# The 512-point transform as four products of 128 columns, with weight rows reordered at load and the instruction order from a table

## The chip, the cores and the metric

One core of one Trainium2 chip. TensorE (PE) multiplies matrices into PSUM, VectorE (DVE), ScalarE (ACT) and GpSimd (POOL) work on tiles, SyncE (SP) issues transfers; ACT and POOL issue some too. Every engine takes its own instructions in program order and waits on semaphores for the others. The metric is the device time of one execution in microseconds (us).

## The reference

A layer norm of x (2048 tokens, model dimension 512), and on it two branches whose sum is added to x: a filter in the frequency domain over both axes, and a gated feed-forward layer with 1792 hidden columns.

```python
def _A_ref(x, w_r, w_i):
    B, S, D = x.shape
    X = jnp.fft.rfft2(x.astype(jnp.float32), axes=(-2, -1))
    W = w_r + 1j * w_i
    X = X * W
    return jnp.fft.irfft2(X, s=(S, D), axes=(-2, -1)).astype(jnp.bfloat16)

def _B_ref(x, w_gate, w_up, w_down):
    g = jnp.einsum("bsd,df->bsf", x, w_gate)
    u = jnp.einsum("bsd,df->bsf", x, w_up)
    h = _gelu(g) * u
    return jnp.einsum("bsf,fd->bsd", h, w_down)

x = A_x
xn = _layernorm(x, axis=-1)
return x + _A_ref(xn, A_w_r, A_w_i) + _B_ref(xn, B_w_gate, B_w_up, B_w_down)
```

## The kernel before

**Order.** The kernel is written as some thousand tasks, each with an engine, a function that issues its instructions, what it reads and writes, an estimated length and a priority. `_Plan.schedule` goes through an assumed clock: whenever an engine is free it takes the ready task with the lowest priority number, gives PSUM banks to it, and so builds one list. `_Prog` turns the list into five queues with semaphore waits. Some tasks have a gate: they start only after a main product (gate/up or down) with at least that priority has started. The priorities come from the dictionary `K` and from the planned places of the main products (`gu_at`, `down_at`); `bonus` favours staying in the same TensorE mode (products on a half or a quarter of the array are modes of their own).

**Front.** Token tiles j = 0 to 15 are taken four at a time (block m). `ln_stat`, `ln_aggr` (L616 to L627) make mean and variance on VectorE and 1/std on POOL; for the first two tiles `ln_first` uses a square root on ScalarE. `ln_norm` (L641) scales a tile of 128 x 512 into `xn`, on VectorE or, for a few, ScalarE. `trans` (L649) transposes it on TensorE and copies it to `xnT[m]`, four quarters of the model dimension (dc) by 512 tokens.

**Transform along the model dimension.** `butter` (L679) folds the four quarters of `xnT[m]` on VectorE: sums and differences of the first and second half, of 1,024 elements each, then the sum and difference of the two quarters of the sums. `unit_D` (L688) multiplies, for each token tile, the folded quarters with constants `fd`: one product of 128 columns each for `f[0]` and `f[1]`, and two of 256 columns that accumulate for `f[2]` and `f[3]`. ScalarE evicts the bank to `xs`. `unit_A` (L707) does the first step along the tokens on half arrays; its results go through the DRAM scratch `scr1` to `tv`. Later `unit_B`, the multiplication with W, `unit_C`, a second scratch, `unit_E` and `unit_F` follow, and VectorE adds the result to `x_sb`.

**Feed-forward.** `gate_up` (L917) makes, for each group fc of 128 hidden columns, four products of 128 x 512 with `wg` and four with `wu`; one product per quarter dc. Blocks 0 and 1 do this directly; blocks 2 and 3 use `gate_up7` (seven products of half size per pair of groups), whose weight sums are made by `w_sums` and `w_sum4` on VectorE. The down products are `down` and `down_last`.

**Loads.** `load_w` (L570) loads a range of column groups of the gate or up weights, all four quarters, with one transfer: 128 partitions, four quarters, the columns. Ranges are 0 to 4, 4 to 8, 8 to 11 and 11 to 14, for gate and up: eight transfers, all on SP's queue (L586 to L607), among those of x, `ident`, `fd` (768 columns) and `am`. The first two tiles of x come half on SP's and half on ACT's queue.

Of the kernel before, what the change touches and what calls it, by code (L numbers as in the profile page):

```python
# [14 lines left out]
D = 512  # L15
# [14 lines left out]
def _constants():  # L30
# [9 lines left out]
    m64 = np.arange(64)[None, :]  # L40
    a0 = tp * (p + 0.5) * (4 * m64) / D
    a2 = tp * (p + 0.5) * (4 * m64 + 2) / D
    im0 = -np.sin(a0)
    im0[:, 0] = (-1.0) ** np.arange(P)
    fo = []
    for c in range(2):
        kodd = np.concatenate([4 * m64[0] + 1, 4 * m64[0] + 3])[None, :]
        a = tp * (p + P * c + 0.5) * kodd / D
        fo += [np.cos(a), -np.sin(a)]
    FD = np.concatenate([np.cos(a0), im0, np.cos(a2), -np.sin(a2)] + fo, 1)  # L50
# [70 lines left out]
    for i, (a, b) in enumerate(((c, s), (-s, c), (-c, -s))):  # L121
# [8 lines left out]
            f16(CM), f16(G.reshape(P, -1)), f16(NA))  # L130

# [83 lines left out]
class _Plan:  # L215
# [37 lines left out]
    def schedule(self):  # L253
# [26 lines left out]
        def refill():  # L280

            c = [i for i in range(8) if owner[i] is None and not isfull[i]]
            t = _Task()
            b = c[-1]
            t.i, t.eng, t.fn, t.r, t.w, t.over = len(T), "pe", (lambda e: self.fill(e, b)), (("wg", 0, 0), ("wg", 0, 1)), (("bank", b),), ()
# [136 lines left out]
def bass_parallel_sum__spectral_gfnet__glu_gated_geglu__prompt_kernel(  # L422
# [25 lines left out]
    with ExitStack() as es:  # L448
# [19 lines left out]
        tmp = area[:, 0:1024].rearrange("p (a c) -> p a c", a=2)  # L468
# [3 lines left out]
        AREA = [("tmp",)] + [("fold", i, k) for i in range(2) for k in range(3)] + [("xs", i) for i in range(4)]  # L472
# [79 lines left out]
        def act(fn, n, r, w, prio, over=(), **kw):  # L552
            return add("act", fn, r=r, w=w, over=over, occ=n / 1200 + 0.055, lat=n / 1200 + 0.24, prio=prio, **kw)
# [13 lines left out]
        def wkey(nm, fs, dcs=(0, 1)):  # L567
# [73 lines left out]
        def ln_norm(j, prio, eng="dve"):  # L641
            if eng == "act":
                act(lambda e: e.activation(xn[:, j % 4, :], x_sb[:, j, :], ACT.Identity, bias=nmr[:, j:j + 1], scale=rstd[:, j:j + 1]), 770,
                    [("x", j, 0), ("x", j, 1), ("nmr", j), ("rstd", j)], [("xn", j % 4)], prio)
                return
            add("dve", lambda e: e.tensor_scalar(xn[:, j % 4, :], x_sb[:, j, :], ag[:, j, 0:1], rstd[:, j:j + 1], ALU.subtract, ALU.mult),
                r=[("x", j, 0), ("x", j, 1), ("ag", j), ("rstd", j)], w=[("xn", j % 4)], occ=0.33, lat=0.47, prio=prio)

        def trans(m, dcs, jjs, prio, eng="dve"):  # L649
# [9 lines left out]
            pe(f, [P] * (len(dcs) * len(jjs)), [("ident",)] + [("xn", jj) for jj in jjs], [("ps", v), ("tr", m, dcs, jjs)], prio, alloc=(v, 1, False))  # L659
# [19 lines left out]
        def butter(m, prio):  # L679
            f = fold[m % 2]  # L680
            k = ("fold", m % 2)
            x = xnT[m]
            dve(lambda e: e.tensor_tensor(tmp, x[:, 0:2, :], x[:, 2:4, :], ALU.add), 1024, xk(m), [("tmp",)], prio, x=2)
            dve(lambda e: e.tensor_tensor(f[:, 2:4, :], x[:, 0:2, :], x[:, 2:4, :], ALU.subtract), 1024, xk(m), [k + (1,)], prio, x=2)
            dve(lambda e: e.tensor_tensor(f[:, 0, :], tmp[:, 0], tmp[:, 1], ALU.add), 512, [("tmp",)], [k + (0,)], prio, x=2)
            dve(lambda e: e.tensor_tensor(f[:, 1, :], tmp[:, 0], tmp[:, 1], ALU.subtract), 512, [("tmp",)], [k + (2,)], prio, x=2)

        def unit_D(j, prio):  # L688
            v = newbank()
            m = j // 4  # L690
            f = fold[m % 2]
            k = ("fold", m % 2)
            c = slice((j % 4) * P, (j % 4 + 1) * P)

            def fn(e):
                o = bank(v).rearrange("p (a r c) -> p a r c", a=2, r=4)
                e.matmul(o[:, :, 0, :], f[:, 0, c], fd[:, 0:128], start=True, stop=False, skip_group_check=True)
                e.matmul(o[:, :, 2, :], f[:, 1, c], fd[:, 128:256], start=False, stop=False, skip_group_check=True)
                e.matmul(o[:, :, 1::2, :], f[:, 2, c], fd[:, 256:512], start=False, stop=False, skip_group_check=True)  # L699
                return e.matmul(o[:, :, 1::2, :], f[:, 3, c], fd[:, 512:768], start=False, stop=True, skip_group_check=True)  # L700
            pe(fn, [P, P, 256, 256], [("fd",)] + [k + (i,) for i in range(3)], [("ps", v)], prio, alloc=(v, 1, False), full=True)
            x4 = xs[j % 4]
            act(lambda e: e.activation(x4.rearrange("p (a c r) -> p a c r", a=2, r=4),
                                       bank(v).rearrange("p (a r c) -> p a c r", a=2, r=4), ACT.Copy, scale=SC_D),
                512, [("ps", v)], [("xs", j % 4)], prio)
# [270 lines left out]
        def x_sums(m, prio):  # L976
# [4 lines left out]
            o = [("xn", i) for i in range(4)]  # L981
            dve(lambda e: e.tensor_tensor(T1, X[:, 0:2, hi], X[:, 0:2, lo], ALU.subtract), 512, xl + xh, [("xt", 0)], prio, x=2, over=o[:1])
            dve(lambda e: e.tensor_tensor(T3, X[:, 2:4, hi], X[:, 0:2, hi], ALU.subtract), 512, xh, [("xt", 2)], prio, x=2, over=o[2:3])
            dve(lambda e: e.tensor_tensor(T2, X[:, 2:4, hi], T1, ALU.subtract), 512, xh + [("xt", 0)], [("xt", 1)], prio, x=2, over=o[1:2])
            dve(lambda e: e.tensor_tensor(T4, X[:, 2:4, lo], T2, ALU.subtract), 512, xl + [("xt", 1)], [("xt", 3)], prio, x=2, over=o[3:])
# [339 lines left out]
        pr = _Prog(nc, es)  # L1325
        pl.emit(pr)
# [51 lines left out]
```

## Time and profile before

| | us |
|---|---|
| median of 3 runs | 178.47 (178.37 to 178.93) |
| the profiled execution | 177.96 |
| its span, first to last instruction | 175.8 |

| engine | busy us |
|---|---|
| PEld (weight loads, overlapping PE) | 124.0 |
| ACT | 115.9 |
| POOL | 60.1 |

The span is what the views of the trace divide; the 2.2 us between it and the execution lie around the instructions. Busy times are sums of records, and on PE and VectorE successive records overlap, so a record's length is longer than the distance to the next one. The granted TensorE clock was 0.999 of full speed. The transfer engines are sixteen; the share that a view gives is their mean. Up to about 22 us they move 270 to 320 GB/s (slices of 4.4 us) at a share near one.

### The profile page before, as it was taken

What the parts mean: (1) busy time and instruction counts of PE and PEld (TensorE: products, weight loads), DVE (VectorE), ACT (ScalarE), POOL (GpSimd) and SP (SyncE); (2) the same over time, 40 slices, a digit from 0 to 9 for tenths busy, and PEclk for the clock granted to TensorE, in tenths of its full rate; (3) what the DMA queues carried; (4) which work ended last, traced back from release to release, by engine and by line L of the source; (5) the groups of instructions that cost most, each with busy time, mean ns of one, the idle gap of its engine ahead of it and who ended that gap; (6) DMA issues with size and microseconds to landing.
All of it is one profiled execution on the core that took longest, in us unless ns stands there. A gap on an engine that the chain in (4) does not pass through costs nothing.

```text
span 175.8 us, 4162 instructions
## 1 busy us (share of the span) xinstructions
PE 169.7 (97%) x1580; PEld 124.0 (71%) x1580; DVE 151.5 (86%) x346; ACT 115.9 (66%) x193; POOL 60.1 (34%) x104
## 2 busy tenths in 40 slices
PE   7989999999999999999999999999999999999992
PEld 2557555557758854444787788887889998888881
DVE  2689799979798755699699899998999999999992
ACT  3625997779973223388853899889928699996200
POOL 2020205458816368888678100004145120000000
PEclk9999999999999999999999999999999999999999
DMA  3999996898867877575898942400022223100013
GB/s 77 308 319 309 267 266 182 242 296 223 192 134 111 165 202 194 146 228 151 205 258 234 237 124 60 123 0 0 6 60 56 69 60 84 39 0 4 0 30 90
DMA packets 20819, 25.26 MB, mean 144 GB/s; under 512 B 3232, under 2 KB 16928, under 8 KB 20544
## 3 DMA queue, kind: packets, MB, share of 16 engines
q1 hardware_dynamic: 17088, 17.21, 36.4%
q0 software_dynamic: 3120, 7.47, 18.2%
q10 hardware_dynamic: 592, 0.33, 0.7%
q8 instruction: 12, 0.20, 0.5%
q14 instruction: 7, 0.06, 0.1%
HBM read 18.70 MB, written 6.29 MB: 142 GB/s over the span
## 4 chain that ended last, share of the span: by engine, by line
PE 83%; DVE 9%; DMA 3%; SPq 2%; issue 1%; DVEq 0%
PE ps L930 25%; PE ps L1105 23%; PE ps L1011 20%; DMA x_sb<-in_A_x_dram 3%; PE ps L826 3%; PE ps L877 2%; PE ps L657 2%; PE ps L855 2%; SPq L560 2%; PE ps L805 1%; DVE hT L1038 1%; DVE hT L1042 1%; PE ps L699 1%; PE ps L700 1%; PE ps L717 1%
## 5 line engine op out<-in xcount | busy, mean ns | idle before, releaser
L930 PE MATMUL ps<-xw,wu 128*128 128x512 f16 (+1 forms) x128 | 29.3, 353 | 0.5 <-DMA wu<-in_B_w_up_dram 0.5
L930 PE MATMUL ps<-xw,wg 128*128 128x512 f16 (+1 forms) x128 | 29.0, 353 | 0.2 <-DVE xw L668 0.2
L934 ACT ACTIVATE gl<-ps 128x512 bf16<-128x512 f32 (+1 forms) x32 | 17.3, 546 | 17.7 <-PE ps L930 17.6
L862 POOL COPY bc<-tv 1x128 bf16<-1x128 bf16 x16 | 8.7, 558 | 39.6 <-ACT bc L861 39.6
L940 DVE TENSOR_TENSOR hT<-ps,gl 128x512 bf16<-128x512 f32 (+1 forms) x26 | 15.4, 602 | 6.5 <-PE ps L930 5.6
L930 PEld LDWEIGHTS ps<-xw,wu 128*128 128x128 bf16 x128 | 12.0, 98 | 11.3 <-DMA wu<-in_B_w_up_dram 0.7
L930 PEld LDWEIGHTS ps<-xw,wg 128*128 128x128 bf16 x128 | 11.9, 98 | 10.6 <-DMA wg<-in_B_w_gate_dram 0.6
L613 POOL DMA_DIRECT2D xw<-in_A_w_r_dram x28 | 16.2, 612 | 7.9 <-PE ps L930 5.0
L1024 ACT ACTIVATE gl<-ps 128x512 bf16<-128x512 f32 x28 | 17.1, 632 | 2.1 <-PE ps L1011 1.2
L613 POOL DMA_DIRECT2D xw<-in_A_w_i_dram x28 | 16.1, 601 | 3.7 <-PE ps L1105 2.5
L1011 PE MATMUL ps<-xn,ws 128*128 128x256 f16 x112 | 16.2, 273 | 0.0
L1011 PE MATMUL ps<-xn,wu 128*128 128x256 f16 x112 | 16.0, 273 | 0.0
L1011 PE MATMUL ps<-xw,wg 128*128 128x256 f16 x112 | 16.0, 273 | 0.0
L1105 PE MATMUL ps<-wd,hT 128*128 128x256 bf16 x112 | 13.6, 273 | 0.0
L617 DVE BATCH_NORM_STATS2 st<-x_sb 128x6 f32<-128x512 bf16 x16 | 10.5, 683 | 3.5 <-DMA x_sb<-in_A_x_dram 3.3
L1105 PE MATMUL ps<-wd,hs 128*128 128x256 f16 (+1 forms) x112 | 13.4, 273 | 0.0
L1105 PE MATMUL ps<-wdt,hs 128*128 128x256 f16 x112 | 13.1, 273 | 0.0
L626 POOL TENSOR_TENSOR rstd<-vpe,mhalf 128x4 f32<-128x4 f32 (+1 forms) x5 | 4.6, 923 | 23.0 <-DVE vpe L624 23.0
L1105 PEld LDWEIGHTS ps<-wd,hT 128*128 128x128 bf16 x112 | 10.6, 98 | 2.1 <-ACT bc L861 0.3
L1105 PEld LDWEIGHTS ps<-wdt,hs 128*128 128x128 f16 x112 | 10.8, 98 | 1.6 <-issue 0.2
L1105 PEld LDWEIGHTS ps<-wd,hs 128*128 128x128 f16 x112 | 10.8, 98 | 1.6 <-DVE mu L1140 0.2
L1011 PEld LDWEIGHTS ps<-xw,wg 128*128 128x128 bf16 x112 | 10.7, 98 | 1.6 <-issue 0.2
(132 smaller groups left out, 381.9 us busy)
## 6 DMA issues: line engine op xcount, KB each, us to landing
scr<-ta SPq DMA_DIRECT2D x32, 64.0 KB, 4.9
tv<-scr SPq DMA_DIRECT2D x8, 256.0 KB, 5.6
scr<-bc SPq DMA_DIRECT2D x16, 128.0 KB, 3.1
area<-scr SPq DMA_DIRECT2D x8, 256.0 KB, 4.2
xw<-in_A_w_r_dram POOLq DMA_DIRECT2D x28, 64.0 KB, 3.8
xw<-in_A_w_i_dram POOLq DMA_DIRECT2D x28, 64.0 KB, 3.6
x_sb<-in_A_x_dram SPq DMA_DIRECT2D x6, 256.0 KB, 10.4
out_dram<-x_sb SPq DMA_DIRECT2D x12, 128.0 KB, 2.3
```

What stands on the lines that cost most here:

```text
L560: return add(eng, lambda e: e.dma_start(dst, src), r=r, w=w, over=over, occ=occ, lat=kb / 1024 / rate, prio=prio, dma=True)
L613: add("pool", lambda e: e.dma_start(dst, src), r=r, w=w, over=over, occ=0.7, lat=kb / 1024 / 0.27, prio=prio, gate=prio, dma=True)
L617: add("dve", lambda e: e.bn_stats(st[:, j, :], x_sb[:, j, :]), r=[("x", j, 0), ("x", j, 1)] + behind, w=[("st", j)], occ=0.6, lat=0.75, pr ...
L626: add("pool", lambda e: e.tensor_tensor(rstd[:, sl], vpe[:, sl], mhalf[:, 0:n], ALU.pow), r=[("vpe", j) for j in js] + [("mhalf",)], w=[(" ...
L826: ins = e.matmul(bank(v, hh)[64 * kl:64 * kl + 64, 256 * z:256 * z + 256], cm[64 * hh:64 * hh + 64, 2 * H + z, kl, i, :], pp[i][64 * hh:64 ...
L862: add("pool", lambda e: e.tensor_copy(z[0:1, 1, :].rearrange("o (b q) -> o b q", b=2), z256[0:1, :].rearrange("o (b j q) -> o b j q", b=2, ...
L930: ins = e.matmul(bank(v)[:, 0:n], w_sb[nm][:, dc, fc * P:(fc + 1) * P], xnT[m][:, dc, c0:c0 + n], start=(dc == 0), stop=(dc == 3))
L934: act(lambda e: e.activation(gl[k][:, 0:n], bank(vs[0])[:, 0:n], ACT.Gelu_apprx_tanh), n, [("ps", v)], [("gl", k)], prio)
L940: dve(lambda e: e.tensor_tensor(o, bank(vs[1])[:, 0:n], gl[k][:, 0:n], ALU.mult), n, [("ps", vs[1]), ("gl", k)], ks, prio + K["dH"])
L1011: ins = e.matmul(bank(v)[:, 256 * q:256 * q + 256], W_, B0[:, dc, :], start=(first and q == 0 and dc == 0), stop=(dc == 1), skip_group_che ...
L1024: act(lambda e: e.activation(gl[k][:], bank(v), ACT.Gelu_apprx_tanh), 512, [("ps", v)], [("gl", k)], prio + K["aG"])
L1105: ins = e.matmul(bank(v)[:, 256 * t:256 * t + 256], A0[:, f, P * t:P * t + P], B0[:, f, :], start=(first and t == 0 and f == 0), stop=(f = ...
```

## The change

Four things change together.

1. The fold goes one step further. `butter` makes the differences' quarters too: it keeps the two half-size sums and differences in `tmp[0]` and `tmp[1]` and makes four results of 512 elements instead of two. `unit_D` is then four products of 128 columns, each with its own quarter of the bank and its own 128 columns of `fd`, which shrinks to 512 columns. The eviction reorders what it writes to `xs`.
2. For the fold to work, quarters 1 and 3 of the model dimension are held from the end, and all quarters with their halves of 64 so placed that rows match. `ln_norm` writes the even quarters with halves of 64 swapped and the odd quarters with each half backwards, in two instructions instead of one. The gate and up weights must have the same row order: `load_w` makes four transfers instead of one, two for the even quarters (64 partitions each, halves swapped) and two for the odd quarters (128 partitions, the source as two halves of 64 rows, each taken backwards). Ranges are now 0 to 4, 4 to 9 and 9 to 14, so 24 transfers instead of eight; the odd quarters of range 0 to 4 go on ACT's queue.
3. `x_sums`, the filling product and the lists of keys follow the new names.
4. After all tasks are made, their priorities and gates are replaced by a table, `ORDER` and `GATES`, in hundredths, and `bonus` becomes 1.0. The planner then builds the list from these.

```diff
-    a0 = tp * (p + 0.5) * (4 * m64) / D
-    a2 = tp * (p + 0.5) * (4 * m64 + 2) / D
...
+    r = np.arange(P)[:, None] ^ 64
+    ae, ao = tp * (r + 0.5) * 2 * m / D, tp * (r + 0.5) * (2 * m + 1) / D
+    im0 = -np.sin(ae)
     im0[:, 0] = (-1.0) ** np.arange(P)
...
+    FD = np.concatenate([np.cos(ae), im0, np.cos(ao), -np.sin(ao)], 1)
...
+ORDER = [
+    0, 30, 315, 100, 0, 0, 63, 0, 63, 189, 378, 315, 252, 189, 126, 252, 441, 504, 126, 465, 1134, 819, 567, 1386,
...
+]
+GATES = {274: 5622, 275: 5293, 276: 4319, 293: 2653, 294: 2740, 295: 2653, 296: 2999, 297: 3261, 298: 5207, 302: 4319, 484: 5871, 485: 7488, 486: 7488, 487:
...
-        def load_w(nm, lo, hi, eng, prio, dcs=(0, 1)):
+        def load_w(nm, lo, hi, eng, prio, odd=None):
-            src = (B_w_gate if nm == "g" else B_w_up).rearrange("(dc p) f -> p dc f", p=P)
+            src = (B_w_gate if nm == "g" else B_w_up).rearrange("(dc i p) f -> i p dc f", i=2, p=P)
             cs = slice(P * lo, P * hi)
-            ds = slice(2 * dcs[0], 2 * dcs[-1] + 2)
-            dma(eng, w_sb[nm][:, ds, cs], src[:, ds, cs], w=wkey(nm, range(lo, hi), dcs), prio=prio, kb=64 * len(dcs) * (hi - lo))
+            n = hi - lo
+            for a in range(2):
+                dma(eng, w_sb[nm][64 * a:64 * a + 64, ::2, cs], src[0][64 - 64 * a:128 - 64 * a, :, cs], w=[(k, f, a) for k, f, _ in wkey(nm, range(lo, hi), (0,))],
+                    prio=prio + 0.01 * a, kb=32 * n)
+            for i in range(2):
+                v = src[1][:, i, cs].rearrange("(a q) f -> a q f", a=2)[:, ::-1]
+                dma(odd or eng, w_sb[nm][:, 2 * i + 1, cs], v, w=[(k, f, 2 + i) for k, f, _ in wkey(nm, range(lo, hi), (0,))], prio=prio + 0.02 + 0.01 * i, kb=32 * n)
...
-        load_w("g", 0, 4, "sp", -99)
+        load_w("g", 0, 4, "sp", -99, "act")
...
-        load_w("u", 0, 4, "sp", -97)
-        load_w("g", 4, 8, "sp", -96)
-        load_w("u", 4, 8, "sp", -95)
+        load_w("u", 0, 4, "sp", -97, "act")
+        load_w("g", 4, 9, "sp", -96)
+        load_w("u", 4, 9, "sp", -95)
...
-        dma("sp", fd[:], c_fd.ap(), w=[("fd",)], prio=-93, kb=192)
+        dma("sp", fd[:, 0:512], c_fd.ap(), w=[("fd",)], prio=-93, kb=128)
...
-        load_w("g", 8, 11, "sp", -92)
-        load_w("u", 8, 11, "sp", -91)
+        load_w("g", 9, 14, "sp", -92)
+        load_w("u", 9, 14, "sp", -91)
...
-        load_w("g", 11, 14, "sp", -88)
-        load_w("u", 11, 14, "sp", -87)
...
+            xq = x_sb[:, j, :].rearrange("p (d i a c) -> p i d a c", i=2, a=2, c=64)
+            o = xn[:, j % 4, :].rearrange("p (d i a c) -> p i d a c", i=2, a=2, c=64)
+            for i, (xi, oi) in enumerate(((xq[:, 0], o[:, 0][:, :, ::-1]), (xq[:, 1], o[:, 1][:, :, :, ::-1]))):
...
-            dve(lambda e: e.tensor_tensor(tmp, x[:, 0:2, :], x[:, 2:4, :], ALU.add), 1024, xk(m), [("tmp",)], prio, x=2)
-            dve(lambda e: e.tensor_tensor(f[:, 2:4, :], x[:, 0:2, :], x[:, 2:4, :], ALU.subtract), 1024, xk(m), [k + (1,)], prio, x=2)
-            dve(lambda e: e.tensor_tensor(f[:, 0, :], tmp[:, 0], tmp[:, 1], ALU.add), 512, [("tmp",)], [k + (0,)], prio, x=2)
-            dve(lambda e: e.tensor_tensor(f[:, 1, :], tmp[:, 0], tmp[:, 1], ALU.subtract), 512, [("tmp",)], [k + (2,)], prio, x=2)
+            t, d = tmp[0], tmp[1]
+            dve(lambda e: e.tensor_tensor(t, x[:, 0:2, :], x[:, 2:4, :], ALU.add), 1024, xk(m), [("tmp", 0)], prio, x=2)
+            dve(lambda e: e.tensor_tensor(d, x[:, 0:2, :], x[:, 2:4, :], ALU.subtract), 1024, xk(m), [("tmp", 1)], prio, x=2)
+            for i, (s, op) in enumerate(((t, ALU.add), (t, ALU.subtract), (d, ALU.subtract), (d, ALU.add))):
+                dve(lambda e, i=i, s=s, op=op: e.tensor_tensor(f[:, i, :], s[:, 0], s[:, 1], op), 512, [("tmp", i // 2)], [k + (i,)], prio, x=2)
...
-                e.matmul(o[:, :, 0, :], f[:, 0, c], fd[:, 0:128], start=True, stop=False, skip_group_check=True)
-                e.matmul(o[:, :, 2, :], f[:, 1, c], fd[:, 128:256], start=False, stop=False, skip_group_check=True)
-                e.matmul(o[:, :, 1::2, :], f[:, 2, c], fd[:, 256:512], start=False, stop=False, skip_group_check=True)
-                return e.matmul(o[:, :, 1::2, :], f[:, 3, c], fd[:, 512:768], start=False, stop=True, skip_group_check=True)
+                for i in range(4):
+                    ins = e.matmul(bank(v)[:, P * i:P * i + P], f[:, i, c], fd[:, P * i:P * i + P], start=(i == 0), stop=(i == 3), skip_group_check=True)
...
+        for t, v in zip(pl.tasks, ORDER):
+            t.prio = v / 100
+            t.gate = GATES[t.i] / 100 if t.i in GATES else None
+        pl.bonus = 1.0
         pl.emit(pr)
```

In the table's order SyncE's first transfers are x tile 0 and tile 1 (first halves), x tiles 2 and 3 (first halves), `ident`, x tiles 2 and 3 (second halves), then the even quarters of wg and wu for groups 0 to 4; the odd quarters of later ranges stand between even ones, x, `fd` and `am`. The last odd load, the first odd quarter of wu for groups 9 to 14, follows x tiles 8 to 11. ACT's queue starts with its halves of x tiles 0 and 1, three odd loads, the first table load, the fourth odd load, and then the square root of tile 0.

More of the change, by code (lines that the diff above doesn't have):

```diff
@@ L467, in bass_parallel_sum__spectral_gfnet__glu_gated_geglu__prompt_kernel @@
         area = sb("area", [P, 8192], F16)
-        tmp = area[:, 0:1024].rearrange("p (a c) -> p a c", a=2)
+        tmp = [area[:, 1024 * i:1024 * i + 1024].rearrange("p (a c) -> p a c", a=2) for i in range(2)]
         fold = [area[:, 2048 + 2048 * i:4096 + 2048 * i].rearrange("p (a c) -> p a c", a=4) for i in range(2)]
@@ L471, in bass_parallel_sum__spectral_gfnet__glu_gated_geglu__prompt_kernel @@
         vv = area[:].bitcast(BF16).rearrange("p (l c) -> p l c", l=32)
[L472 removed]
+        AREA = [("tmp", 0), ("tmp", 1)] + [("fold", i, k) for i in range(2) for k in range(4)] + [("xs", i) for i in range(4)]
         ta = sb("ta", [P, 2048], F16)
@@ L658, in f @@
                 return ins
-            pe(f, [P] * (len(dcs) * len(jjs)), [("ident",)] + [("xn", jj) for jj in jjs], [("ps", v), ("tr", m, dcs, jjs)], prio, alloc=(v, 1, False))
+            pe(f, [P] * (len(dcs) * len(jjs)), [("ident",)] + [("xn", jj, i) for jj in jjs for i in range(2)], [("ps", v), ("tr", m, dcs, jjs)], prio, alloc=(v, 1, False))
             w = len(jjs) * P
@@ L980, in x_sums @@
             T1, T2, T3, T4 = xt
[L981 to L985, printed above, removed]
+            o = [[("xn", i, a) for a in range(2)] for i in range(4)]
+            dve(lambda e: e.tensor_tensor(T1, X[:, 0:2, hi], X[:, 0:2, lo], ALU.subtract), 512, xl + xh, [("xt", 0)], prio, x=2, over=o[0])
+            dve(lambda e: e.tensor_tensor(T3, X[:, 2:4, hi], X[:, 0:2, hi], ALU.subtract), 512, xh, [("xt", 2)], prio, x=2, over=o[2])
+            dve(lambda e: e.tensor_tensor(T2, X[:, 2:4, hi], T1, ALU.subtract), 512, xh + [("xt", 0)], [("xt", 1)], prio, x=2, over=o[1])
+            dve(lambda e: e.tensor_tensor(T4, X[:, 2:4, lo], T2, ALU.subtract), 512, xl + [("xt", 1)], [("xt", 3)], prio, x=2, over=o[3])
         un = [0]
```

34 lines of the change are left out of this document (14 added, 20 removed), and 51 rows, old and new, of tables (GATES, ORDER).

## The prediction

> **What bounds the kernel now.** I read the page's busy shares first, then the chain of work that ended last in order of time, then the stages (windows), and last the timeline and the transfers of the first 26 us.
>
> ```profile
> span 175.8 us, 4162 instructions
> ...
> PE 169.7 (97%) x1580; PEld 124.0 (71%) x1580; DVE 151.5 (86%) x346; ACT 115.9 (66%) x193; POOL 60.1 (34%) x104
> ...
> PE   7989999999999999999999999999999999999992
> ```
>
> ```profile
> 3.67 4.67 DMA x_sb<-in_A_x_dram
> 8.41 0.71 DVE st L617
> ...
> 12.84 4.53 PE ps L930 x36
> ...
> 17.48 0.11 PE ps L699
> 17.59 0.11 PE ps L700
> ...
> 24.96 0.89 PE ps L657 x16
> ...
> 172.46 0.42 DVE x_sb L1125
> ```
>
> The chain has start, times and length. To 12.84 us it runs through loads and the first layer norms; from 12.84 to 172.46 it is TensorE nearly without a hole (159.6 us), and then 3.3 us of last addition and store. So TensorE columns count one to one, everything else only where TensorE must wait for it. The profiled execution took 177.96 us, 2.2 us more than its span, and the median of the runs shown is 178.47, another 0.5 us up; I add 2.7 us to a span.
>
> **The transform (removed).** A unit of `unit_D` is two products of 128 columns and two of 256. The 256s take 0.11 each on the chain; sixteen transposes of 128 columns take 0.89 us, 0.056 each. Before: 2 x 0.056 + 2 x 0.11 = 0.33 us. After: 4 x 0.056 = 0.22 us. Over 16 units 1.76 us goes. A rule against it: the Trainium skill, TensorE: Matmul & The Clock Gate, section Back-to-back issue gap, gives 81 ns for sustained 128-column products with their weight loads. By that a unit would take 0.32 us and nothing would be gained; the 0.89 us for sixteen, each with its own weight load, speaks against it here, and I keep 0.056.
>
> **Vector work (added).** `butter` grows by two half-size operations per block, eight in all; the windows' columns are length, PE, PEld, DVE, ACT and POOL busy, clock, DMA share, GB/s:
>
> ```profile
> 14.44 0.41 DVE L685 TENSOR_TENSOR area<-area 128x512 f16<-128x512 f16 x1
> 14.77 0.42 DVE L686 TENSOR_TENSOR area<-area 128x512 f16<-128x512 f16 x1
> ```
>
> ```profile
> 12.80:26.00 13.20, 13.16 (x111) 8.66 (x111) 12.14 (x34) 10.42 (x21) 1.15 (x1) 1.00 1.07 279
> 26.00:40.00 14.00, 14.00 (x100) 7.54 (x99) 12.94 (x38) 10.58 (x17) 7.26 (x10) 1.00 0.85 244
> 40.00:53.00 13.00, 12.94 (x123) 8.89 (x122) 11.50 (x25) 11.82 (x20) 8.09 (x15) 1.00 0.77 178
> ```
>
> ```profile
> L668 DVE COPY xw<-ps 128x256 f16<-128x256 f16 x1 | 0.3, 293 | 0.0
> ```
>
> A record of 0.41 us is followed 0.33 us later by the next, so 0.08 us of each overlaps: 8 x 0.33 = 2.6 us. Twelve layer-norm scalings on VectorE become 24 of 256 elements; the nearest row (293 ns, so 0.21 us in a row) gives 2 x 0.21 - 0.33 = 0.09 each, 1.1 us. Four on ScalarE (815 ns, L643) become halves, some 0.2 us more each by its 384 ns rows of 256, 0.8 us. Writing backwards costs nothing: L887 does it in 414 ns, L886 without in 427. Cover: from 12.8 to 53 us VectorE is busy 36.6 of 40.2 us, but 97 records x 0.08 = 7.8 us of that is overlap, so 11.4 us are free, against 3.7 added. Cost zero; without the cover, 3.7 us. The eviction of `unit_D` now writes every second element; between nothing and a doubling of its 606 ns (16 x 0.6 = 9.7 us of ScalarE, which has 7.4 us idle in those windows). I take nothing: L887 shows no price for another stepped write.
>
> **Order (moved).** I read the table's numbers as the order on each engine. Passages through the half-array mode of `unit_A` become six instead of four; one costs about 0.1 us to enter and 0.1 to leave (in the timeline the last product of one starts at 47.23 and takes its 0.11, the next begins at 47.44). That is +0.4 us. At the front SyncE issues the transfers of x tiles 2 and 3 third and fifth instead of sixth and seventh, and ScalarE's queue gets three weight loads before its table load and one before its first square root:
>
> ```profile
> 2.09 1.28 ACT L579 ACT_TABLE_LOAD   x1 [2.09 <-issue]
> ...
> 4.36 0.29 ACT L632 ACTIVATE vpe<-ag,epst 128x1 f32<-128x1 f32 x1 [0.77 <-DVE ag L631]
> ...
> 7.46 1.91 PE L930 MATMUL ps<-xw,wg 128*128 128x256 f16 x16 [0.18 <-DVE xw L668]
> ```
>
> An issue on that queue takes 0.66 us (two in 1.32), so the square root slips to about 5.9 us, the first transposes by 1.2 us and the first gate product from 7.46 to about 8.5. Against that x tiles 2 and 3 come near 6.2 instead of 8.34, and TensorE need not wait until 12.84 to run closed. Net between -0.6 and +0.1 us; I take -0.3. SyncE's issues rise by 10 on net to the end of the loads, at 0.5 us each, behind a queue that waits for bandwidth anyway.
>
> **Weight loads (split): the term that decides.** Eight loads become 24: for each of six ranges two of even quarters (64 rows outermost) and two of odd quarters. An odd load's source is written as two halves, each of 64 rows taken backwards, so its description has an outermost count of **two**, against 128 at the destination.
>
> ```profile
> DMA packets 20819, 25.26 MB, mean 144 GB/s; under 512 B 3232, under 2 KB 16928, under 8 KB 20544
> ...
> tv<-scr SPq DMA_DIRECT2D x8, 256.0 KB, 5.6
> ...
> wg<-in_B_w_gate_dram SPq DMA_DIRECT2D x2, 512.0 KB, 5.4
> ```
>
> ```profile
> 4.40:8.80 4.40, 4.22 (x31) 2.40 (x30) 2.93 (x9) 2.68 (x6) 0.00 (x0) 1.00 1.00 309
> ```
>
> No transfer of before has fewer than 16 pieces outermost. The narrowest, `tv<-scr` and its sibling on `area` (16 transfers, 16 rows of 16 KB), account for 256 of the 275 packets of 8 KB or more: a transfer is cut at its rows and the rows are dealt out. How one is dealt whose two sides begin with 2 and 128 is not shown. The bounds: over all sixteen engines (the odd loads cost what the old ones did) or over two. I take two, because a common division of both sides at their outermost count has only two parts, and every full-rate row has a count that sixteen divides. The Trainium skill, DMA: Bandwidth & Descriptors, section Why a DMA increments its semaphore by 16 and not by 1, says the same: the number of engines is the largest up to 16 that divides the slowest dimension of both sides, and on these queues the lowest-numbered ones are used. No run here shows it yet.
>
> Price over two engines. Up to the last odd load of wu (the second quarter of groups 9 to 13), each of those two carries half of 1,792 KB of odd quarters, 896 KB, and a sixteenth of the rest (x 1,536, even quarters 1,792, am 256, fd 128, ident 32: 3,744 KB), 234 KB: 1,130 KB. An engine's pace: 309 GB/s at a share of 1.00 is 19.3 GB/s, 53 ns a KB; the highest slice of the first 26 us, 389 GB/s, is 24 GB/s, 42 ns:
>
> ```profile
> GB/s 0 0 0 147 197 138 61 296 389 323 173 304 377 373 372 358 353 369 233 233 231 234 309 357 335 325 347 286 204 238 220 271 329 339 359 356 207 251 176 211
> ```
>
> I take 47 ns, between them, as two engines have the memory to themselves: 53 us. Transfers start moving near 2.5 us; with 0.5 for the signal the last lands at 56. In the table's order TensorE may do ahead of it only 32 transposes (1.8), 17 products of 512 columns (0.86 each, 14.7), four units D (0.9) and two A (0.9): 18.3 us, of which before had done 4.4 at 12.84 (16 transposes, 32 half products). So after 56 us there remains 159.6 - 1.8 + 0.4 - (18.3 - 4.4) = 144.3 us. **Sum:** 56 + 144.3 + 3.3 = 203.6 us of span, + 2.7 = 206.3; I say **206**. By 42 ns it is 201, by 53 ns 213. Within that wait TensorE starves in steps: the first gate quarters late, then each range; the work between is short enough not to add up beyond the last one. Products after an idle start ran 0.43 us apart in the warm-up (2.06, 2.48, 2.91) instead of 0.22, so restarts may add 1 to 3 us: 216 at the top, 197 at the bottom if the waits of before (about 1 us) and some of the loads' tail go too.
>
> **Rivals.**
> *Faster: the odd loads are spread over sixteen.* Then loads are bandwidth bound as before (346 KB an engine by the same point, landing near 20 us, ahead of the product that needs it) and the rest counts: -1.8 + 0.4 - 0.3 = -1.7, **176.8 us**. For it: every load row of before runs at full rate. Against: none has such a shape.
> *No gain: as before that, but the front loses.* The square root's delay of 1.5 us reaches TensorE whole, because the x tiles meet ScalarE's new loads on the same engines: -1.8 + 0.4 + 1.5, **178.6 us**. Against: VectorE waits for x tiles 2 and 3 in before until 8.41, later than any of this.
> *Slower by little: only the first four odd loads matter.* If engines take up odd loads from several queues at once and the later ones stay ahead, TensorE starts after 4 x 64 KB on an engine, 12 us, plus as much of the other queue, near 26 us instead of 10: **193 us**.
>
> **Numbers.** Two engines: 0.82, with its own range 197 to 216. Only the front loads: 0.05. Spread, faster: 0.10. Spread, no gain: 0.03. The predicted time is the likeliest, 206; the range 192 to 216 leaves out the two spread cases and little more. 0.3% of 178.5 is 0.5 us, about what can be told from no change here: faster 0.10, same 0.03, slower 0.87.
>
> **What would show it.** Right: the odd wg and wu loads take 10 to 30 us to land, the DMA row falls from nines to a few tenths over the first 55 us with well under 150 GB/s, the PE row has holes there and the chain names DMA for wg and wu, while a unit D takes 0.22 us and the stage after 60 us looks like before. Wrong: DMA at nines to 20 us, TensorE closed from about 9 us, and a time near 177; then a count of two outermost does not confine a transfer.

## The result, and the profile after

The changed kernel takes **210.24 us** (median of 4 runs, 210.06 to 210.76) against 178.5 for the kernel before on the same chip: a ratio of 1.177, with a 95% interval of 1.173 to 1.182. The forecast was 206, with 192 to 216 as its range.

The page of the profiled execution after (210.16 us; 40 slices of 5.2 us):

```profile
span 208.2 us, 4199 instructions
...
PE 176.0 (85%) x1580; PEld 124.8 (60%) x1580; DVE 155.2 (75%) x366; ACT 118.6 (57%) x197; POOL 59.0 (28%) x104
...
PE   7350669507949999999999999999999999999993
...
PEclk9955559975999999999999999999999999999999
DMA  3434125255859978586756799754000055020013
```

The same last row of the kernel before (slices of 4.4 us):

```profile
DMA  3999996898867877575898942400022223100013
```

TensorE's row has holes over the first twelve slices, some 62 us, and none later. The granted clock is half in five of these slices, and the transfer engines, at nines up to 26 us in the kernel before, stand at one to five tenths over the first ten. The same stretch in the view of the transfers, first 70 us, 40 slices of 1.75 us:

```profile
DMA  0557517111581111169311141689238897428999
GB/s 0 153 141 212 146 46 204 47 49 49 142 205 52 49 49 52 35 157 214 84 49 55 45 119 57 194 211 251 68 107 241 181 329 222 123 65 315 344 314 239
```

Read the two rows together. Wherever the share is one tenth, the rate is 35 to 57 GB/s, most often 49. The highest slice of before, 389 GB/s over sixteen engines, is 24 a piece; 49 is twice that. So two engines work and fourteen stand idle. That was the forecast's deciding step, and the Trainium skill, DMA: Bandwidth & Descriptors, section Why a DMA increments its semaphore by 16 and not by 1, has the rule that these numbers agree with: the largest number of engines, up to sixteen, that divides the outermost count of both sides.

The trace also records each write to the semaphore that tells of a transfer's landing, though no view prints them. An even load has sixteen writes. Each of the twelve odd loads has three: one soon after its issue and two at the end (the last one, issued at 46.70, has them at 47.68, 59.27 and 59.70). And nearly every ordinary load has fourteen early writes and two late ones: for the x tiles issued at 46.05 fourteen by 50.40, the last two at 55.97 and 56.22. So it is one and the same pair of engines that all odd loads queue on, and every other transfer has two of its sixteen parts behind them.

TensorE's waits (total, times, longest), and its timeline at their ends (start, length, what; in brackets the idle time before and what ended it):

```profile
PE ps L991 <- DMA wg<-in_B_w_gate_dram: 16.5, 3, 9.0
PE ps L718 <- DVE rstd L690: 5.1, 1, 5.1
PE ps L991 <- DMA wu<-in_B_w_up_dram: 5.0, 2, 2.7
```

```profile
21.91 3.57 PE L991 MATMUL ps<-xw,wg 128*128 128x256 f16 x16 [7.25 <-DMA wg<-in_B_w_gate_dram]
...
48.17 1.86 PE L991 MATMUL ps<-xw,wg 128*128 128x512 f16 x4 [9.00 <-DMA wg<-in_B_w_gate_dram]
...
59.94 1.02 PE L991 MATMUL ps<-xw,wu 128*128 128x512 f16 x4 [2.68 <-DMA wu<-in_B_w_up_dram]
...
72.17 1.07 PE L718 MATMUL ps<-ident,xn 128*128 128x128 f16 x16 [0.33 <-DVE xn L707]
```

The first gate product starts at 21.91 instead of 7.46, and its sixteen records of 256 columns span 3.57 us where before they spanned 1.91: half the clock. The last odd load of wu lets TensorE go on at 59.94; from there to the end of the span are 148.3 us. Two instruction queues suffered too. SyncE's and ScalarE's own queues (an issue is mostly 0.6 us; the longest single one among the loads of the kernel before is 2.72):

```profile
11.44 6.14 SPq L613 DMA_DIRECT2D wg<-in_B_w_gate_dram  x1
...
20.14 9.55 SPq L613 DMA_DIRECT2D wg<-in_B_w_gate_dram  x2
...
35.67 7.21 SPq L613 DMA_DIRECT2D wu<-in_B_w_up_dram  x2
```

```profile
5.36 5.27 ACTq L613 DMA_DIRECT2D wu<-in_B_w_up_dram  x1
...
10.67 0.29 ACT L689 ACTIVATE vpe<-ag,epst 128x1 f32<-128x1 f32 x1 [3.89 <-issue]
```

Seven issues on SyncE's queue and one on ScalarE's are held for 3 to 6 us (the longest is the one at 11.44; the lines with x2 have two issues). They are not those of odd loads alone: the one at 11.44 is of an even load, and one below is of x tiles. Whatever follows in that queue waits too, whether or not it needs those weights: ScalarE's first square root (10.67 instead of 4.36) and, on SyncE, `fd`, `am` and the x tiles. The chain of waits that ended last runs through such a bystander:

```profile
47.28 3.81 SPq L613
...
51.13 10.52 DMA x_sb<-in_A_x_dram
...
62.28 0.68 DVE area L746
```

An x load is issued late and lands at 61.65, two of its parts behind the last odd load (fourteen of its semaphore writes come by 55.50, the last two at 60.76 and 61.65). VectorE has its statistics at the head of its queue until then, and the folds, layer norms and transposes of 72.17 stand behind it.

### The profile page after: what moved, and what is told of

The parts are those of the page before. It is cut to its first block, busy times and chain, and to the rows that moved or that the text cites. A ratio compares the mean times of both kernels' runs of the same rounds, so it can differ in the third digit from the quotient of the medians.

```text
span 208.2 us, 4199 instructions
## 1 busy us (share of the span) xinstructions
PE 176.0 (85%) x1580; PEld 124.8 (60%) x1580; DVE 155.2 (75%) x366; ACT 118.6 (57%) x197; POOL 59.0 (28%) x104
## 2 busy tenths in 40 slices
DMA packets 19883, 25.20 MB, mean 121 GB/s; under 512 B 3320, under 2 KB 15992, under 8 KB 19608
## 4 chain that ended last, share of the span: by engine, by line
PE 59%; SPq 24%; DVE 10%; DMA 5%; issue 2%
SPq L613 24%; PE ps L1072 20%; PE ps L1166 17%; PE ps L991 12%; DMA x_sb<-in_A_x_dram 5%; PE ps L887 2%; DVE hs L1155 2%; DVE st L674 1%; PE ps L916 1%; PE ps L938 1%; PE ps L866 1%; PE ps L718 1%; PE ps L760 1%; DVE xn L707 1%; PE ps L1181 1%
## 5 line engine op out<-in xcount | busy, mean ns | idle before, releaser
L991 PE MATMUL ps<-xw,wg 128*128 128x512 f16 (+1 forms) x128 | 29.9, 378 | 16.5 <-DMA wg<-in_B_w_gate_dram 16.5
L923 POOL COPY bc<-tv 1x128 bf16<-1x128 bf16 x16 | 7.9, 494 | 44.3 <-ACT bc L922 44.1
L1072 PE MATMUL ps<-xw,wg 128*128 128x256 f16 x112 | 16.5, 273 | 0.0
L1166 PE MATMUL ps<-wd,hT 128*128 128x256 bf16 x112 | 13.5, 273 | 0.0
L764 ACT ACTIVATE area<-ps 128x512 f16<-128x512 f32 x16 | 10.5, 749 | 2.4 <-PE ps L760 2.2
```

What stands on the lines that cost most here:

```text
L764: act(lambda e: e.activation(x4.rearrange("p (a c r) -> p r a c", a=2, r=2), bank(v).rearrange("p (r a c) -> p r a c", a=2, r=2), ACT.Copy ...
L923: add("pool", lambda e: e.tensor_copy(z[0:1, 1, :].rearrange("o (b q) -> o b q", b=2), z256[0:1, :].rearrange("o (b j q) -> o b j q", b=2, ...
L991: ins = e.matmul(bank(v)[:, 0:n], w_sb[nm][:, dc, fc * P:(fc + 1) * P], xnT[m][:, dc, c0:c0 + n], start=(dc == 0), stop=(dc == 3))
L1072: ins = e.matmul(bank(v)[:, 256 * q:256 * q + 256], W_, B0[:, dc, :], start=(first and q == 0 and dc == 0), stop=(dc == 1), skip_group_che ...
L1166: ins = e.matmul(bank(v)[:, 256 * t:256 * t + 256], A0[:, f, P * t:P * t + P], B0[:, f, :], start=(first and t == 0 and f == 0), stop=(f = ...
```

## The experiments

All are compared with runs of the kernel before on the same chip; a ratio is to these runs.

**Is it the shape of the loads? Sixteen parts, four parts.** One number in `load_w`:

```diff
-                v = src[1][:, i, cs].rearrange("(a q) f -> a q f", a=2)[:, ::-1]
+                v = src[1][:, i, cs].rearrange("(a q) f -> a q f", a=16)[:, ::-1]
```

> The changed kernel with the source of each odd load written as sixteen groups of 8 rows (each backwards) instead of two of 64; bytes, number of transfers, queues and table stay. The odd quarters' weight rows come in another order, so the feed-forward products are of other rows. Theory (a transfer is dealt over as many engines as divide the outermost counts of both sides): sixteen engines, the first 50 us run at 200 GB/s and more, the loads land by 22 us, 176 to 178 us. Rival (the reading backwards, or the number of 24 loads, is what is slow): 205 to 211 us as after.

Measured: **179.6 us** (178.71 to 181.18, 12 runs), ratio 1.005 (1.001 to 1.009). Its transfers in the first 60 us (slices of 1.5 us):

```profile
DMA  0389999999999999999999999995975888654467
GB/s 0 114 249 259 258 250 241 263 233 227 264 203 267 269 264 275 252 230 210 234 353 377 361 350 295 336 227 103 263 197 139 210 235 86 135 131 96 100 155 234
```

All sixteen engines, and 30.6 us gone, with the same bytes, the same number of transfers and the same table. In its trace every odd load has sixteen semaphore writes. Nothing else of the change can carry these 30.6 us. But the rest is not the gain that the rival promised (176.8) either; that is taken up below. With a=4:

> The same with four groups of 32 rows; again another row order in the odd quarters. Theory: four engines, plateaus near 4 x 24 = 97 GB/s where two gave 47 to 49; up to the last odd load each of the four carries 448 + 234 = 682 KB instead of 1,130, at the 24 GB/s seen 29 us, landing near 33 us, some 6 us after the table's order needs it: 181 to 188 us. Rival (backwards or number of loads): 205 to 211 us.

Measured: **194.76 us** (194.13 to 195.21), ratio 1.089 (1.083 to 1.095). The order of the three is right, the size is not. Its first 70 us:

```profile
DMA  0557892862594235899999863629799999859797
GB/s 0 152 139 180 216 209 85 231 145 94 158 229 130 99 108 145 237 203 208 207 193 233 216 160 123 180 85 313 252 302 302 187 169 203 268 159 269 145 96 166
```

The plateaus now lie at 85 to 108 GB/s and two to three tenths: four engines. Each odd load has one early semaphore write and four at its end. In its trace the last odd load of wu lets TensorE go at 44.52, and from there to the end of its span (192.8) are 148.3 us, to the tenth what the changed kernel has after 59.94. So the time follows the landing of that load one to one, and it was the landing that I set too early, in both. At the plateaus' pace (42 ns a KB) four engines with a quarter of 1,792 KB and the sixteenth of the rest, 682 KB, need 28.6 us and two with 1,130 KB need 47.5; with 3 us of start and signal that is 31.6 and 50.5. TensorE goes on 12.9 and 9.4 us later. The few engines did not stop in between: once the transfers have started no slice of either view falls under the digit of their share (one and two tenths), and the next odd load was always issued before the one ahead of it had landed (in the changed kernel the load that landed at 47.83 was issued at 31.58, and the next, which landed at 52.02, at 35.67). It is their pace that varied. An odd load of 160 KB is 80 KB for each of the two. One landed at 37.63, 3.18 us after the odd load issued just ahead of it (40 ns a KB, for the most part in slices of 49 and 55 GB/s). Another, at 47.83, needed 4.81 us (60 ns a KB), while other engines moved data too, 194 and 211 GB/s in all. From 3 us to the last landing (59.70, and 44.27 with a=4) it is 50.2 ns a KB for the pair with its 1,130 KB each and 60.5 for the four with their 682. So the few engines are slower when the others work as well; that they then share the memory is the likely reason, and no run shows it by itself.

**And the shape alone, in the kernel before?** `load_w` of the kernel before with three transfers a range, all on SyncE's queue: both even quarters as before, each odd quarter as two halves backwards (without the `rearrange` and the backward slice in the control).

```diff
-            dma(eng, w_sb[nm][:, ds, cs], src[:, ds, cs], w=wkey(nm, range(lo, hi), dcs), prio=prio, kb=64 * len(dcs) * (hi - lo))
+            dma(eng, w_sb[nm][:, ::2, cs], src[:, ::2, cs], w=[(k, f, 0) for k, f, _ in wkey(nm, range(lo, hi), (0,))], prio=prio, kb=64 * n)
+            for i in range(2):
+                v = src[:, 2 * i + 1, cs].rearrange("(a q) f -> a q f", a=2)[:, ::-1]
+                dma(eng, w_sb[nm][:, 2 * i + 1, cs], v, w=[(k, f, 1 + i) for k, f, _ in wkey(nm, range(lo, hi), (0,))], prio=prio + 0.02 + 0.01 * i, kb=32 * n)
```

> The kernel before with only the loads changed: even quarters in one transfer per range, odd quarters in one transfer each, with the source as two halves of 64 rows backwards, all on SyncE's queue; 24 transfers in before's own order. The odd quarters' rows are in another order than the reference has. Theory: two engines again, x tiles 12 to 15 and the last up weights come near 50 to 55 us, 195 to 206 us, without any of the transform's change or the table. Rival (the table's order or the transform brings the loss): 178 to 180 us.

> Control to the run before it: the same 24 transfers, in the same places, with the odd quarters' 128 rows in their plain order, outermost count 128. The computation is the reference's. Theory: within 1 us of before, 178 to 179.5 us, as issuing is hidden behind bandwidth. Rival (more transfers on the queue cost): 181 us or more.

Measured: **210.61 us** (210.36 to 210.69), ratio 1.178 (1.170 to 1.185), and for the control **179.66** (178.72 to 180.19, 10 runs), ratio 1.005 (1.002 to 1.008). The shape by itself makes the whole loss; that the time comes within 0.4 us of the changed kernel's is chance, since order and path differ. Both forecasts were somewhat low: what stands behind the odd loads in their queue was not in the first, and the control shows that 24 transfers in place of eight cost about 1.2 us by themselves. Where the time goes in b2 is in its TensorE timeline:

```profile
12.23 3.57 PE L933 MATMUL ps<-xw,wg 128*128 128x256 f16 x16 [5.08 <-DMA wg<-in_B_w_gate_dram]
...
34.79 0.29 PE L700 MATMUL ps<-fd,area 128*128 128x128 f16 x1 [6.47 <-DMA fd<-c_fd]
...
51.72 1.87 PE L933 MATMUL ps<-xw,wu 128*128 128x512 f16 x4 [4.96 <-DVE vpe L627]
```

The longest wait is for `fd`, a load of 128 full rows that has nothing wrong with it. It stood behind held issues in SyncE's queue (issued at 26.51, in the kernel before at 7.25), and then with two of its parts on the busy pair: fourteen had landed by 31.30, the last two came at 34.28 and 34.74.

**Is the confinement a property of the shape alone?** The changed kernel with the twelve odd loads issued by GpSimd:

```diff
-                dma(odd or eng, w_sb[nm][:, 2 * i + 1, cs], v, w=[(k, f, 2 + i) for k, f, _ in wkey(nm, range(lo, hi), (0,))], prio=prio + 0.02 + 0.01 * i, kb=32 * n)
+                dma("pool", w_sb[nm][:, 2 * i + 1, cs], v, w=[(k, f, 2 + i) for k, f, _ in wkey(nm, range(lo, hi), (0,))], prio=prio + 0.02 + 0.01 * i, kb=32 * n)
```

> The kernel after, with all twelve odd loads issued from GpSimd's queue instead of SyncE's and ScalarE's; shapes unchanged. Theory (the shape of a transfer, not the queue that issues it, sets how many engines carry it, and always the same two): within some 8 us of after, 202 to 214 us; SyncE's own loads may no longer be held up behind the odd ones, which can give back up to 8. Rival (the software queue deals a transfer out over its own choice of engines): 180 to 195 us.

Measured: **196.75 us** (195.45 to 197.41), ratio 1.099 (1.094 to 1.105): 13.5 us under the changed kernel, and outside what my theory allowed. Its page:

```profile
DMA  3899999986996957559478897460000334110013
GB/s 88 171 179 185 151 185 189 179 184 185 234 251 148 180 117 153 133 135 195 111 234 210 216 241 206 127 150 0 2 5 0 75 90 108 31 26 0 3 27 81
DMA packets 21587, 25.24 MB, mean 130 GB/s; under 512 B 6176, under 2 KB 17312, under 8 KB 21312
```

The engines are all busy from 5 us on, with the same two-part shape. So it falls that such loads always go to the same two engines; that holds on SyncE's and ScalarE's queues. The section of the Trainium skill named above has this too: on GpSimd's queue a transfer that is split k ways takes k neighbouring engines from a place that moves round from transfer to transfer. The mean share fits that; a single engine isn't shown. It is no cure, though. The engines are busy at 180 GB/s instead of 250 to 270, and packets under 512 bytes went from 3,320 to 6,176. Smaller packets at the same share are the likely reason for the 17 us that remain over a16; no run separates them from the late `ident` and first weights (TensorE waited 3.7 us for `ident` and 8.2 us for a load of wg here).

**Where did the transform's 1.7 us go?** With the loads out of the way the change should have won. First attempt: the changed kernel with one plain transfer a range, table kept for everything else; then with the removed columns put back, with the eviction written in a row, and without the table. In these and in the `transform` kernels below, it is the gate and up products whose weight rows then don't match the columns' order.

```diff
-            for a in range(2):
-                dma(eng, w_sb[nm][64 * a:64 * a + 64, ::2, cs], src[0][64 - 64 * a:128 - 64 * a, :, cs], w=[(k, f, a) for k, f, _ in wkey(nm, range(lo, hi), (0,))],
...
+            dma(eng, w_sb[nm][:, :, cs], src[:, :, cs], w=wkey(nm, range(lo, hi)), prio=prio, kb=32 * n)
```

> The kernel after, with every range of groups of wg and wu loaded by one transfer of 128 plain rows (6 transfers instead of 24, table kept for all the rest). The rows of the quarters then stand in another order than the transform's constants take. Theory (the four products of 128 do save 1.8 us, and sixteen-row loads gave it back through 18 more transfers at the front, as the control with plain rows lost 1.2 us): 176.5 to 177.8 us, first gate product before 8.2 us. Rival (the saving does not exist, or other parts of the change, the vector operations and the stretched eviction, eat it): 178.3 to 179.6 us even with few loads.

> The kernel of plain, with six products of 128 columns in unit_D instead of four (the last two done twice, so those outputs are doubled): the columns that the change removed are put back. Theory (columns count one to one on TensorE, 0.056 us a product): 16 x 2 x 0.056 = 1.8 us over plain. Rival one (the units stand where TensorE has slack): under 0.5 us over plain. Rival two (a product of 128 with its own weight load costs 81 ns, as the Trainium skill's TensorE: Matmul & The Clock Gate, section Back-to-back issue gap, has it): 2.6 us over plain.

> The kernel of plain, with the eviction of unit_D written in a row instead of to every second element (the columns of the transform then stand in another order). The eviction goes back from about 750 ns to about 610. Theory (ScalarE's 16 x 0.14 = 2.2 us hide behind TensorE except where one product waits for the area, 0.3 us in the trace): 0 to 0.5 us under plain. Rival (the longer eviction is what gives the saving back): 1 us or more under plain.

> The kernel of plain without the table: the order comes from the list scheduler's own due times, as in the kernel before. Theory (the table is worth nothing that stands out here): within 0.6 us of plain. Rival one (the table carries the gain): 1 us or more over plain. Rival two (the table is what gives the saving back: four loads on ScalarE's queue, six passages of the half-array mode): 1 us or more under plain.

Measured: 185.81 us (184.59 to 187.03), 188.01, 185.04 and 186.9, ratios 1.037 (1.032 to 1.043), 1.045, 1.033 and 1.042. The forecast for plain missed by 8 us and took the base away from the other three, whose differences to plain are +2.2, -0.8 and +1.1 us: the new base is 6 us slower than a16, with fewer transfers. VectorE's timeline of plain, and TensorE's:

```profile
18.23 0.69 DVE L672 BATCH_NORM_STATS2 st<-x_sb 128x6 f32<-128x512 bf16 x1 [5.45 <-DMA x_sb<-in_A_x_dram]
```

```profile
21.26 1.03 PE L989 MATMUL ps<-xw,wg 128*128 128x256 f16 x4 [4.69 <-ACT gl L993]
```

VectorE's queue had the statistics of x tile 4 at its head and stood 5.45 us until it landed; the products `hT` behind it free the banks that TensorE waited for. In plain this x tile was issued behind five of the six weight loads and landed at 18.2; in a16 the wait ahead of that block's first statistics is 1.00 us. The table alone is not the reason, since the hole is there without it too. The edit itself may be: it keeps `kb=32 * n`, from which the planner reckons how long a transfer takes, for transfers of four times that size, so its list counts on weights and x tiles that come too early. No run changes that number alone; the kernels below give it right (128 KB a group), and their longest hole is 1.78 us. The hole at this place is 4.7 us in plain, 6.6 in plain_six, 6.0 in plain_evict, and 5.8 in plain_no_table, so the differences between the four say nothing on columns, eviction or table: inconclusive.

Second attempt, a cleaner base: the kernel before, its loads and its scheduler, with the transform alone changed; with the columns put back; and with the statistics placed as in before.

```diff
-                for i in range(4):
+                for i in (0, 1, 2, 3, 2, 3):
```

```diff
-                ln_stat(4 * m + i, a + i)
+                ln_stat(4 * m + i, a + i, [("xn", 2, 1)] if m == 2 else [])
```

> The kernel before with the transform alone changed (four products of 128, the two more vector operations per block, the layer norms in halves, the eviction to every second element): loads, their order and the scheduler as before, no table. The rows of the quarters then stand in another order than the transform's constants take. Theory (1.76 us of columns go, and VectorE's and ScalarE's extra work stays hidden): 176.3 to 177.6 us, that is 1.2 to 2.2 us under the runs of before beside it. Rival (the extra work on VectorE and ScalarE, 3.7 and 3 us, comes through at TensorE's waits for evictions and layer norms): 178 us or more, no gain.

> The kernel of transform, with six products of 128 columns in unit_D instead of four (the last two done twice, so those outputs are doubled), in the same order. Theory (columns count one to one): 1.8 us over transform, about the time of before. Rival (the units stand where TensorE waits anyway): under 0.6 us over transform.

Measured: **179.89 us** (179.09 to 181.16), ratio 1.007 (1.002 to 1.011), and 181.07, ratio 1.012 (1.007 to 1.017). The transform alone is no gain; it is 0.3 to 2 us slower. The theory's own half holds on TensorE: in the trace of transform four units start at 18.09 and the next work at 18.99, 0.90 us, where before they take from 17.21 to 18.53, 1.32 us (the first two lines below are transform, the others before). That is 1.7 us over the kernel.

```profile
18.09 1.07 PE L754 MATMUL ps<-fd,area 128*128 128x128 f16 x16
18.99 1.03 PE L985 MATMUL ps<-xw,wu 128*128 128x512 f16 x4
```

```profile
17.21 0.22 PE L697 MATMUL ps<-fd,area 128*128 128x128 f16 x1
...
18.53 1.03 PE L930 MATMUL ps<-xw,wu 128*128 128x512 f16 x4
```

With two more products each, the time rose by 1.2 us, in the right direction, but the two intervals overlap. What eats the saving showed first as one hole, 1.78 us in front of the transposes at 30.65, behind a wait of VectorE for x tiles:

> The kernel of transform, with the statistics of x tiles 8 to 11 placed behind the first layer norms of tiles 4 to 7 on VectorE, as they stand in the kernel before. In the trace of transform VectorE waited 2.46 us at the head of its queue for those x tiles, the layer norms stood behind, and TensorE lost 1.78 us in front of the transposes at 30.65. Theory (the transform does save 1.7 us, and this wait gave it back): 177.2 to 178.3 us, 1.2 to 2.2 us under transform, and no hole over 0.6 us ahead of the second block's transposes. Rival (the longer vector work is the cause, and the wait only moves to another place): within 0.6 us of transform, with another hole of a microsecond or more.

Measured: **180.38 us** (179.61 to 181.51, 12 runs), ratio 1.009 (1.006 to 1.013), against 179.89 with the hole. The hole went down to 0.23 us and nothing was won in the median; the profile that showed the hole was the slowest of transform's six runs (181.16), and how long it is in the others isn't recorded. TensorE's waits in this kernel:

```profile
PE ps L712 <- DVE xn L701: 1.0, 3, 0.5
PE ps L754 <- DVE area L742: 0.6, 2, 0.4
PE ps L1160 <- DVE hT L995: 0.4, 1, 0.4
PE ps L910 <- DVE hT L1093: 0.4, 1, 0.4
PE ps L1160 <- DVE wdt L1129: 0.3, 1, 0.3
PE ps L985 <- DVE hT L995: 0.3, 1, 0.3
```

Six lines of waits for VectorE, 3.0 us, at layer norms, folds and evictions; with one lesser it is 3.2 us after the first instruction, against 1.0 us in the kernel before. That is 2.2 of the 3.6 us by which transform_stats misses the saving (1.9 over before instead of 1.7 under); for the rest these lines have no place. The rival holds in the main: the wait moves to other places, if not as one hole of a microsecond. The groups of the changed kernel show what grew, and the three lines of before under them what it replaced (count, busy us, mean ns):

```profile
L764 ACT ACTIVATE area<-ps 128x512 f16<-128x512 f32 x16 | 10.5, 749 | 2.4 <-PE ps L760 2.2
...
L707 DVE TENSOR_SCALAR xn<-x_sb,ag,rstd 128x256 f16<-128x256 bf16 x24 | 6.9, 339 | 0.7 <-POOL rstd L683 0.7
...
L704 ACT ACTIVATE xn<-x_sb,nmr,rstd 128x256 f16<-128x256 bf16 x8 | 4.3, 592 | 0.0
```

```profile
L703 ACT ACTIVATE area<-ps 128x512 f16<-128x512 f32 x16 | 8.4, 610 | 0.8 <-PE ps L700 0.8
...
L646 DVE TENSOR_SCALAR xn<-x_sb,ag,rstd 128x512 f16<-128x512 bf16 x12 | 4.7, 412 | 0.4 <-POOL rstd L626 0.3
...
L643 ACT ACTIVATE xn<-x_sb,nmr,rstd 128x512 f16<-128x512 bf16 x4 | 3.0, 815 | 0.0
```

Half a layer norm costs 82% of a whole one on VectorE and 73% on ScalarE. The eviction's growth is that of its write: in plain_evict, written in a row, it takes 600 ns, in plain 746.

## Why the prediction held, and where it was off

**The shape (two of sixteen): right, and shown.** Plateaus of 49 GB/s, two late semaphore writes of each odd load, the loss in b2, its disappearance in a16. The rival that spreads the loads has a16 as its case.

**The landing: right mechanism, size 4 us short.** I had 53 us of transfer and a landing at 56; TensorE went on at 59.94. The load itself landed at 59.70. The term that was mis-sized is the pace: 47 ns a KB, taken between the bounds of 42 and 53, was 50.2 in the mean, and 3.2 ns on 1,130 KB are 3.6 us. The pair did have the memory to itself on the plateaus, at 42, but not while the other fourteen engines moved their parts. For a4 I took the quick bound of 42 for the whole way, where 60.5 was measured; that made the forecast 7 us too low.

**What is left after it: right.** 144.3 + 3.3 = 147.6 us forecast, 148.3 found, in two kernels. The forecast's 2.7 us around the span were 2.0 to the median. 203.6 + 3.9 + 0.7 + 2.0 is the 210.2.

**Which wait ends last: only half seen.** I priced the queue's odd loads and took the others as mere bystanders ("behind a queue that waits for bandwidth anyway"). In the trace the last x tiles of the block land 1.7 us after the last odd load is in use, held in the queue and with two parts behind it on the pair, and the chain goes through them. Had the odd load come at 56 and these x tiles as they did, TensorE would have run dry before the transposes of 72.17. That is read from the trace, not tried.

**The front.** The square root was forecast at 5.9 and came at 10.67, as ScalarE's fourth odd load held its queue for 5.27 us, not 0.66. It hid behind the gate weights, which came only at 21.91. What the front costs with spread loads is in a16's trace: square root at 5.34, first gate product at 9.05 instead of 7.46, first unit D at 18.22 instead of 17.21. So the net of -0.3 us that the sum took was 1.0 us the other way.

**The transform's columns: right** (1.7 us; 0.056 us a product). The Trainium skill's 81 ns, TensorE: Matmul & The Clock Gate, section Back-to-back issue gap, is not borne out for this stream: sixteen products with their own weight loads take 0.90 us.

**Vector work at nothing: wrong, and hidden by the larger loss.** VectorE's busy time rose by 3.7 us, as summed, but the cover of 11.4 us was never there. The busy time of a view counts overlapping records once: in the lines above, 24 records of 339 ns are 8.1 us and the view gives 6.9. (So busy times are not sums of records, as the note under the table of busy times ahead of the prediction has it.) The overlap of 7.8 us was thus taken off twice; free were 40.2 - 36.6 = 3.6 us, no more than the 3.7 added. The prediction's price without the cover is the one that came near: transform, with that work and without the shape, is 1.3 us slower instead of 1.7 faster, 3.0 us in all. So the rival's 176.8 was wrong too; with spread loads 179.6 was measured, which lies near the second rival's 178.6. The late front that this rival gives as the reason is there, but with 1.0 us only a part of it; the vector work, which it took as free, is the other. That the added instructions stand in order in front of evictions and folds that TensorE waits for is read from the waits of transform_stats. Whether it is the length of these instructions or their place in the queue isn't settled: in transform_stats VectorE itself waits 2.4 us for POOL's 1/std, against 0.9 before.

**The stepped eviction at nothing: wrong by 0.14 us each**, 2.2 us of ScalarE. a16 shows one wait of TensorE on it, 0.33 us. **The table** was not separated from the rest.

## What to carry to other kernels

Before a load is rewritten for a new row order, write down the outermost count of both its sides: from SyncE's or ScalarE's queue, two there meant two transfer engines here, and four meant four; the share beside GB/s shows it. A slow transfer is paid by all that stands behind it, in its queue and on its engines, so price the bystanders as well. Before free time of an engine is counted as cover, find out whether the view's busy time counts overlapping records once or twice. And even true free time, summed over a stage, is no cover for an instruction that stands in front of one that the critical engine waits for.

## What the hardware showed that was not expected

An instruction that only issues a transfer, an ordinary one too, can hold its queue for 3 to 6 us instead of 0.6 while the transfers ahead of it crawl on two engines; a full-rate load then still has two of its sixteen parts on these engines, some 6 us after the other fourteen (50.40 and 56.22 for x tiles). Two engines move a KB in 42 ns each when alone and needed 60 when the others worked too. The same two-part shape, issued from GpSimd, keeps all engines busy (180 GB/s), but in nearly twice as many packets under 512 bytes. And half a layer norm, in rows of 64 that are written backwards or swapped, takes 339 ns for 256 elements on VectorE, where the row that I had taken as nearest, a copy, was 293; how much of that is the order of writing and how much the other operation isn't separated.
